# An adaLN linear-attention block with a token mixer: first modulation vectors and small inputs laid out in tiles of 128 partitions, half of their sum moved to TensorE

## The chip, the core and the metric

The kernel runs as one program on one core of a Trainium2 chip. The metric is the device time of one execution in microseconds (us); the median of three runs before the change is 452.39 us (452.24 to 452.70).

## The reference, cut to what matters

A block of 2048 tokens (S) by 448 channels (D). A condition vector c gives six modulation vectors; the first two, sa and ca, shape the input of the attention.

```python
mod = (silu(c) @ w_mod).reshape(1, 6, 1, 448)
sa, ca, ga, sb, cb, gb = (mod[:, i] for i in range(6))
h = layernorm(x) * (1 + ca) + sa
x = x + ga * linear_attention(h, wqkv, wo)        # 16 heads of 28, phi = elu + 1
h = layernorm(x) * (1 + cb) + sb
x = x + gb * mixer(h, w1, b1, w2, b2)             # W2 gelu(W1 h + b1) + b2 over the tokens
```

Inputs and output are float32. c has 448 numbers, w_mod is 448 x 2688, wqkv 448 x 1344.

## The kernel before, in words

The program is one long manual schedule: each engine runs its instructions in the order in which the Python code emits them, and waits only for data. Tokens are handled in 16 tiles of 128 (index t), channels in chunks of 128 (three full ones and one of 64, chunk index ch). Matrix products are done in float32 for the first tile (`project0`) and afterwards as sums of float32r products of a high and a low part (`split`, `project`, `a_outer`). Then come the token mixer's first product (w1, lines 740 to 742) and its second (w2, a Strassen-like scheme, lines 932 and 933).

What matters here is the head, everything before the first product of tile 0.

- **Loads.** SyncE (SP) issues them one after the other: c (line 99, four bytes apiece, to 112 partitions x 4), x tile 0 (`load_x`, line 104), four pieces of w_mod for vector 1, which is ca (`load_mod`, line 111, 112 partitions x 448 each), four pieces for vector 0, which is sa, x tile 1, then wqkv's k part (`load_qkv`, lines 119 and 122, the last 64 rows twice, each in a transfer of its own), x tile 2, wqkv's q part, x tiles 3 to 6. There are eight semaphores for these loads, used in turn, so that each load waits for the landing of the eighth load before it.
- **silu(c).** ScalarE (ACT) takes the exponential (`ec`, line 147), VectorE (DVE) does the rest (lines 149 to 151, result `sc`), and makes the broadcast columns `scb` of the last two pieces (line 425).
- **Modulation vectors.** For vector j, DVE multiplies the first three of the four pieces by their column of `sc` and adds them (`mod_acc`, lines 160 and 162, one pass of 112 x 448 for each). TensorE (PE) then sums over the partitions (`mod_sum`, line 177): one product of the fourth piece with its `scb`, and one of the accumulated tile with ones. Vector 1 is copied out of PSUM with 1 added (`mod_out`, line 156, tile `mods[1]`). Vector 0 stays in PSUM (`sap`) and is read from there by tile 0 and tile 1; it is copied out later, behind the work of tile 1.
- **Tile 0.** `a_stats` (lines 276 to 289; the power of -0.5 is on GpSimd, POOL), `a_norm_a` (line 294, needs `mods[1]`), `a_cols` (line 432, multiplies by the reciprocal deviation and adds sa, in two column pieces of 256 and 192), transposes on PE (`a_first`, line 437), copies by ACT (`a_copy`, line 442), and the first product kp (`project0`, line 448). Between its second and third chunk `project0` puts the transposes of tile 1 (`a_transpose`, line 312), which need `a_norm_a(1)`, `a_norm_b(1)` (line 300) and a small copy (`a_dup`, line 304).
- **Fillers.** `keep_warm` (line 141) issues 128 x 128 products of ones whose result nobody reads: 12 + 10 ahead of the first modulation sum, 5 ahead of the second, then twice 2. 

In code order, the head ends so (the names in the lines below recur in the steps):

```python
    a_stats(0)
    mod_acc(1, 3)
    keep_warm(WARM2)
    mod_out(1, mod_sum(1, 3))
    mod_acc(0, 3)
    keep_warm(WARM3)
    a_norm_a(0)
    moments1 = a_moments(1)
    a_stats(1, moments1)
    sap = mod_sum(0, 3)
```

From tile 0's first product on, the loop over tiles goes on with `project`, `a_outer`, `a_pk_parts` (POOL's accumulating DMAs at lines 376, 399 and 405) and, in iteration 4, the loads of wo, wqkv's v part, b1 and b2 (lines 582 and 584, four bytes apiece).

Of the kernel before, what the change touches and what calls it, by code (L numbers as in the profile page):

```python
# [32 lines left out]
QS = {0: 2, 4: 2}  # L33
WARM = 12
WARM2, WARM3 = 10, 5
ACT_STATS = ()
# [7 lines left out]
@with_exitstack  # L44
def block_kernel(ctx: ExitStack, tc: tile.TileContext, x, wqkv, wo, w1, b1, w2, b2, c, wmod, out):
    nc = tc.nc
# [25 lines left out]
    def bank(name):  # L72
        return psum.tile([P, 512], F32, name=name, tag="bank")
# [23 lines left out]

    c_sb = cst.tile([G, 4], F32, name="c_sb")
    nc.sync.dma_start(c_sb, c.rearrange("o (k p) -> p (o k)", p=G))
    X = [None] * NT  # L100

    def load_x(t):
        X[t] = slot(f"x{t}")
        nc.sync.dma_start(X[t], xf[t * P:(t + 1) * P, :])
# [10 lines left out]
    def load_qkv(j, new=None):  # L115
        new = new or slot
        for ch in range(3):
            raw_w[j, ch] = new(f"wr{j}_{ch}")
            nc.sync.dma_start(raw_w[j, ch], wqkv[ch * P:(ch + 1) * P, j * D:(j + 1) * D])
        raw_w[j, 3] = new(f"wr{j}_3")  # L120
        for h in range(2):
            nc.sync.dma_start(raw_w[j, 3][h * 64:(h + 1) * 64, :], wqkv[384:448, j * D:(j + 1) * D])

    load_x(0)
    load_mod(1)
    load_mod(0)
    load_x(1)
    load_qkv(1)
    load_x(2)
# [9 lines left out]
    def keep_warm(n):  # L139
        for i in range(n):  # L140
            nc.tensor.matmul(warm[:, :P], ones, ones, start=True, stop=True)
# [3 lines left out]

    ec = cst.tile([G, 4], F32, name="ec")
    nc.scalar.activation(ec, c_sb, AF.Exp, scale=-1.0)
    sc = cst.tile([G, 4], F32, name="sc")
    nc.vector.tensor_scalar_add(ec, ec, 1.0)
# [7 lines left out]

    def mod_acc(j, n=4):
        acc = (tslot if j == 5 else slot)(f"acc{j}", parts=G)
        nc.vector.tensor_scalar_mul(acc, wm[j, 0], sc[:, 0:1])  # L160
        for k in range(1, n):
            nc.vector.scalar_tensor_tensor(acc, wm[j, k], sc[:, k:k + 1], acc, op0=ALU.mult, op1=ALU.add)
        macc[j] = acc

    def mod_part(j, k):
        if k == 0:
            macc[j] = (tslot if j == 5 else slot)(f"acc{j}", parts=G)
            nc.vector.tensor_scalar_mul(macc[j], wm[j, 0], sc[:, 0:1])
        else:
            nc.vector.scalar_tensor_tensor(macc[j], wm[j, k], sc[:, k:k + 1], macc[j], op0=ALU.mult, op1=ALU.add)  # L170

    def mod_sum(j, n=4):
        ps = bank(f"modp{j}")
        todo = [(scb[:, (k - 2) * P:(k - 1) * P], wm[j, k]) for k in range(n, 4)]
        todo.insert(1, (ones[:G, :], macc.pop(j)))
        for k, (a, b) in enumerate(todo):
            nc.tensor.matmul(ps[:, :D], a, b, start=(k == 0), stop=(k == len(todo) - 1))
        return ps

# [242 lines left out]

    scb = cst.tile([G, 2 * P], F32, name="scb")
    for k in range(2):
        nc.vector.tensor_scalar_mul(scb[:, k * P:(k + 1) * P], ones[:G, :], sc[:, k + 2:k + 3])

# [3 lines left out]
    def a_cols(c0, c1, sa):  # L430
        h = hs[0]
        nc.vector.scalar_tensor_tensor(h[:, c0:c1], h[:, c0:c1], st[0][1], sa[:, c0:c1], op0=ALU.mult, op1=ALU.add)

# [30 lines left out]
    keep_warm(2)  # L464
    a_cols(0, 256, sap)
    a_cols(256, D, sap)
    tps[0] = bank("tp0")
# [10 lines left out]
    w_high(1, 1)  # L478
    a_norm_b(1, sap[:, :D])
    a_dup(1)  # L480
# [7 lines left out]
    w_low(1, 3)  # L488
    mod_out(0, sap)
    a_stats(2)  # L490
# [45 lines left out]
    for t in range(3, NT):  # L536
# [581 lines left out]

_INS = ['A_x', 'A_wqkv', 'A_wo', 'B_w1', 'B_b1', 'B_w2', 'B_b2', 'c', 'w_mod']
_OUTS = [((1, S, D), 'float32')]  # L1120


# [20 lines left out]
```

## Time and profile before

| | |
|---|---|
| median of 3 runs | 452.39 us (452.24 to 452.70) |
| profiled execution, first to last instruction (span) | 451.1 us |
| median of the runs over that span | 1.3 us |
| PE busy | 444.3 us, 98% of the span |
| DVE, ACT, POOL busy | 352.0, 255.7, 109.0 us |
| DMA, mean over the span | 137 GB/s |

The profile shows one execution on the hardware. A row names the line, the engine, the operation and its tiles; a chain of waits goes back from the last instruction to what released each step. PE rows overlap, since products are pipelined, and each float32 product appears as two rows. The profiled execution gives no whole time of its own besides its span; differences are formed on the span and carried over to the median.

### The profile page before, as it was taken

Reading aid. Unit: us, or ns where it says so; the run is one execution under the profiler, and the core shown is the slowest. Engines: PE = TensorE matmul, PEld = TensorE weight load, DVE = VectorE, ACT = ScalarE, POOL = GpSimd, SP = SyncE. Lnnn points to the kernel's source line nnn. Section 1 sums busy time; section 2 is a strip of 40 time slices with the busy share of each in tenths; the row PEclk is TensorE's granted clock in tenths of the full one; section 3 lists DMA queues with packets and bytes.
Section 4 is the critical chain, followed back from the end, with each engine's and each line's share of the span. In section 5 each row is a group of like instructions: output and inputs, shape, how many; then the busy total and the mean of one; then the engine's idle time right before and its main releaser. Section 6 shows DMA issues by size and latency. Waiting matters only on the chain.

```text
span 451.1 us, 7324 instructions
## 1 busy us (share of the span) xinstructions
PE 444.3 (98%) x2396; PEld 408.5 (91%) x2396; DVE 352.0 (78%) x767; ACT 255.7 (57%) x568; POOL 109.0 (24%) x186
## 2 busy tenths in 40 slices
PE   8999999999999999999999999999999999999996
PEld 7589999889899999999999999999999999999996
DVE  5797797789799899897559686639697888978873
ACT  2659877655666576767675454326554547356531
POOL 2124575520013345554300000000110211302101
PEclk9999999999999999999999999999999999999999
DMA  8959899995200002322317553317987569975334
GB/s 216 293 146 190 143 194 238 188 246 159 72 0 2 23 25 80 82 50 50 117 27 221 178 173 116 103 62 221 279 207 182 98 186 211 191 192 99 57 85 62
DMA packets 62246, 61.63 MB, mean 137 GB/s; under 512 B 9152, under 2 KB 54784, under 8 KB 62208
## 3 DMA queue, kind: packets, MB, share of 16 engines
q1 hardware_dynamic: 53136, 46.94, 35.8%
q0 software_dynamic: 9072, 14.23, 19.9%
q8 instruction: 19, 0.31, 0.3%
q14 instruction: 19, 0.16, 0.1%
HBM read 42.34 MB, written 7.34 MB: 110 GB/s over the span
## 4 chain that ended last, share of the span: by engine, by line
PE 86%; POOL 4%; issue 4%; DVE 2%; DMA 1%; SPq 1%; ACT 0%; POOLq 0%; DVEq 0%
PE y L932 14%; PE up L742 10%; PE up L741 10%; PE up L740 10%; PE op L689 9%; PE qp L333 7%; PE y L933 7%; PE cacc L420 3%; PE kp L333 3%; PE yp L740 2%; PE yp L742 2%; PE yp L741 2%; PE tq L673 2%; POOL xl L376 1%; DMA wm<-in_w_mod_dram 1%
## 5 line engine op out<-in xcount | busy, mean ns | idle before, releaser
L742 PE MATMUL up<-h2h,pl 128*128 128x448 f32 x224 | 81.3, 363 | 0.0
L741 PE MATMUL up<-h2l,ph 128*128 128x448 f32 x224 | 81.2, 362 | 0.0
L740 PE MATMUL up<-h2h,ph 128*128 128x448 f32 x224 | 80.8, 361 | 0.0
L741 PEld LDWEIGHTS up<-h2l,ph 128*128 128x128 f32 x224 | 42.1, 188 | 3.1
L740 PEld LDWEIGHTS up<-h2h,ph 128*128 128x128 f32 x224 | 41.9, 187 | 3.0
L742 PEld LDWEIGHTS up<-h2h,pl 128*128 128x128 f32 x224 | 42.1, 188 | 2.4
L77 DVE TENSOR_TENSOR pl<-pr,ph 128x512 fp32r<-128x512 f32 (+1 forms) x60 | 36.3, 616 | 8.6 <-ACT ph L76 6.1
L76 ACT ACTIVATE ph<-pr 128x512 fp32r<-128x512 f32 (+1 forms) x60 | 32.8, 569 | 13.2 <-PE up L741 6.8
L894 POOL DMA_DIRECT2D a<-a x12 | 11.2, 1070 | 110.3 <-PE yp L742 97.0
L952 POOL DMA_DIRECT2D out_dram<-yt x12 | 10.5, 873 | 85.7 <-DVE yt L943 57.3
L689 PE MATMUL op<-wph,pth 112*128 112x448 f32 x64 | 24.5, 382 | 0.0
L420 PE MATMUL cacc<-pkh,xh 128*128 128x448 f32 x64 | 24.3, 379 | 0.0
L689 PE MATMUL op<-wpl,pth 112*128 112x448 f32 x64 | 23.2, 363 | 0.0
L420 PE MATMUL cacc<-pkl,xh 128*128 128x448 f32 x64 | 23.2, 362 | 0.0
L689 PE MATMUL op<-wph,ptl 112*128 112x448 f32 x64 | 23.1, 362 | 0.0
L938 ACT ACTIVATE cc<-y 128x448 f32<-128x448 f32 x18 | 9.8, 544 | 23.3 <-PE y L933 23.3
L333 PE MATMUL kp<-wh,hl 128*128 128x448 f32 x60 | 21.7, 367 | 1.1 <-DVE hl L77 1.1
L333 PE MATMUL kp<-wh,hh 128*128 128x448 f32 x60 | 21.6, 366 | 0.0
L333 PE MATMUL qp<-wh,hh 128*128 128x448 f32 x60 | 21.6, 366 | 0.0
L333 PE MATMUL qp<-wh,hl 128*128 128x448 f32 x60 | 21.4, 363 | 0.0
L677 ACT ACTIVATE pth<-tq 112x512 fp32r<-112x512 f32 x16 | 9.6, 599 | 20.5 <-PE tq L673 17.7
L289 POOL TENSOR_TENSOR rs<-ve,mhalf 128x1 f32<-128x1 f32 x16 | 14.3, 896 | 24.5 <-DVE ve L287 23.9
(214 smaller groups left out, 1309.8 us busy)
## 6 DMA issues: line engine op xcount, KB each, us to landing
pr<-in_B_w_dram SPq DMA_DIRECT2D x48, 256.0 KB, 3.1
a<-in_B_w_dram SPq DMA_DIRECT2D x24, 256.0 KB, 5.0
wm<-in_w_mod_dram SPq DMA_DIRECT2D x24, 196.0 KB, 4.9
a<-in_B_w_dram SPq DMA_DIRECT2D x24, 192.0 KB, 5.0
x<-in_A_x_dram SPq DMA_DIRECT2D x16, 224.0 KB, 4.5
pk<-pk POOLq DMA_DIRECT2D x12, 224.0 KB, 5.0
out_dram<-x SPq DMA_DIRECT2D x12, 224.0 KB, 2.0
out_dram<-yt POOLq DMA_DIRECT2D x12, 224.0 KB, 4.2
```

Source lines behind the costliest of these rows:

```text
L76: nc.scalar.activation(hi, full, AF.Copy)
L77: nc.vector.tensor_sub(lo, full, hi.bitcast(F32))
L289: nc.gpsimd.tensor_tensor(rs, ve, mhalf[:, 0:1], op=ALU.pow)
L333: nc.tensor.matmul(o, a[:, ch * P:(ch + 1) * P], b, start=(n == 0), stop=(n == 10))
L420: nc.tensor.matmul(cacc[ch][:, :D], a[:, s], b, start=(t == 0 and i == 0), stop=(t == NT - 1 and i == len(todo) - 1))
L689: nc.tensor.matmul(opb[t][:, :D], a[:, s], b, start=(n == 0), stop=(n == 11))
L740: nc.tensor.matmul(ps[:, :D], hi[:, sl], mh, start=first, stop=False)
L741: nc.tensor.matmul(ps[:, :D], hi[:, sl], ml, start=False, stop=False)
L742: nc.tensor.matmul(ps[:, :D], lo[:, sl], mh, start=False, stop=last)
L894: nc.gpsimd.dma_start(w, a, accum_op=ALU.add)
L932: nc.tensor.matmul(ps[:, :D], h[:, s], w, start=opens and r == 0, stop=False, skip_group_check=True)
L933: nc.tensor.matmul(ps[:, :HD], l[:, s], wh, start=False, stop=closes and r == PAIRS - 1, skip_group_check=True)
```

## The change

The host lays out five inputs anew, and the kernel reads them in that form.

- c comes as 128 x 8: columns 0 to 2 are its chunks of 128, column 3 is the last 64 numbers twice, columns 4 to 7 are the four pieces of 112 (for the later vectors). Its load is issued by ACT, no longer by SP.
- The parts of w_mod for vectors 1 and 0 come as one array `first` of 2 x 128 x 1600: three chunks of 128 rows x 448, and a fourth in which the last 64 rows stand as 128 partitions x 256 (columns 0 to 255 on partitions 0 to 63, columns 256 to 447 on partitions 64 to 127, filled with zeros). SP loads vector 1 first, then x tile 0, vector 0, the first k chunk, x tile 1, the rest.
- wqkv comes as tiles of 128 x 448, its last 64 rows twice in one tile, hence one load in place of two; b1 and b2 come as 128 x 14 and 128 x 16.
- PE now sums chunks 0 and 1 of each vector directly (`spread`, `first_mm`); DVE handles chunk 2 and the folded chunk 3 alone (`first_acc`: one multiplication and two passes on 64 partitions). Vector 0 is summed in two PSUM banks (256 and 192 columns), each with its own piece of `first_acc`.
- Tile 1's moments stand behind `a_cols` instead of ahead of it, and `a_norm_b(1)` reads `mods[0]`, which ACT copies out of the two banks ahead of it; the later copy of vector 0 is gone.
- The fillers are 9, 3 and 2, in place of 12, 10 and 5.

```diff
-WARM = 12
-WARM2, WARM3 = 10, 5
+WARM = 9
+WARM2, WARM3 = 3, 2
...
-    c_sb = cst.tile([G, 4], F32, name="c_sb")
-    nc.sync.dma_start(c_sb, c.rearrange("o (k p) -> p (o k)", p=G))
+    c_sb = cst.tile([P, 8], F32, name="c_sb")
+    nc.scalar.dma_start(c_sb, c)
...
+    def load_first(j):
+        for k in range(4):
+            w = D if k < 3 else 256
+            wm[j, k] = slot(f"wm{j}_{k}", w)
+            nc.sync.dma_start(wm[j, k], wfirst[j, :, k * D:k * D + w])
+
+    load_first(1)
     load_x(0)
-    load_mod(1)
-    load_mod(0)
+    load_first(0)
+    load_qkv(1, chs=(0,))
     load_x(1)
-    load_qkv(1)
+    load_qkv(1, chs=(1, 2, 3))
...
+    def spread(k):
+        nc.vector.tensor_scalar_mul(scb[:, k * P:(k + 1) * P], ones, sc[:, k:k + 1])
+
+    def first_acc(j, c0, c1, rows):
+        if j not in macc:
+            macc[j] = slot(f"acc{j}")
+        acc = macc[j]
+        nc.vector.tensor_scalar_mul(acc[:, c0:c1], wm[j, 2][:, c0:c1], sc[:, 2:3])
+        for r in rows:
+            p, (d0, d1) = slice(r * 64, (r + 1) * 64), ((0, 256), (256, D))[r]
+            nc.vector.scalar_tensor_tensor(acc[p, d0:d1], wm[j, 3][p, :d1 - d0], sc[p, 3:4], acc[p, d0:d1],
+                                           op0=ALU.mult, op1=ALU.add)
+
+    def first_mm(j, k, ps, c0, c1):
+        a, b = (scb[:, k * P:(k + 1) * P], wm[j, k]) if k < 2 else (ones, macc[j])
+        nc.tensor.matmul(ps[:, :c1 - c0], a, b[:, c0:c1], start=k == 0, stop=k == 2)
...
+    ca = bank("modp1")
+    first_mm(1, 0, ca, 0, D)
+    first_mm(1, 1, ca, 0, D)
+    first_acc(1, 0, D, (0, 1))
+    keep_warm(WARM2)
+    first_mm(1, 2, ca, 0, D)
+    mod_out(1, ca)
+    del macc[1]
     a_stats(0)
-    mod_acc(1, 3)
-    keep_warm(WARM2)
-    mod_out(1, mod_sum(1, 3))
-    mod_acc(0, 3)
+    saps = [(bank("modp0"), 0, 256), (bank("modq0"), 256, D)]
+    for k in (0, 1):
+        for sap in saps:
+            first_mm(0, k, *sap)
+    a_norm_a(0)
+    for r, sap in enumerate(saps):
+        first_acc(0, *sap[1:], (r,))
     keep_warm(WARM3)
-    a_norm_a(0)
+    for sap in saps:
+        first_mm(0, 2, *sap)
+    del macc[0]
+    a_cols(0, 256, saps[0][0])
+    a_cols(256, D, saps[1][0])
     moments1 = a_moments(1)
     a_stats(1, moments1)
-    sap = mod_sum(0, 3)
-    keep_warm(2)
-    a_cols(0, 256, sap)
-    a_cols(256, D, sap)
...
     w_high(1, 1)
-    a_norm_b(1, sap[:, :D])
+    mods[0] = cst.tile([P, D], F32, name="mod0")
+    for ps, c0, c1 in saps:
+        nc.scalar.activation(mods[0][:, c0:c1], ps[:, :c1 - c0], AF.Copy)
+    a_norm_b(1)
...
-    mod_out(0, sap)
...
-            nc.sync.dma_start(b1c, b1.rearrange("(k p) -> p k", p=P))
+            nc.sync.dma_start(b1c, b1)
-            nc.sync.dma_start(b2c, b2.rearrange("(k p) -> p k", p=P))
+            nc.sync.dma_start(b2c, b2)
```

PE's head before, from its first filler to the first product of tile 0 (modp are the banks of the modulation sums, acc the tiles that DVE accumulates, wm_3 the fourth pieces, tp and kp tile 0's transposes and product):

```order
L141 MATMUL warm<-ones 128x128 x22
L177 MATMUL modp_185<-wm_3_100,scb 128x448
L177 MATMUL modp_185<-acc_171,ones 128x448
L141 MATMUL warm<-ones 128x128 x5
L177 MATMUL modp_209<-wm_3_108,scb 128x448
L177 MATMUL modp_209<-acc_190,ones 128x448
L141 MATMUL warm<-ones 128x128 x2
L437 MATMUL tp_216<-ident,h_199 128x128 x3
```

The same stretch of PE with the change (wm_0 and wm_1 are chunks 0 and 1; modp_179 and modq_180 the two banks of vector 0):

```order
L145 MATMUL warm<-ones 128x128 x9
L179 MATMUL modp_158<-wm_0_92,scb 128x448
L179 MATMUL modp_158<-wm_1_94,scb 128x448
L145 MATMUL warm<-ones 128x128 x3
L179 MATMUL modp_158<-acc_161,ones 128x448
L179 MATMUL modp_179<-wm_0_102,scb 128x256
L179 MATMUL modq_180<-wm_0_102,scb 128x192
L179 MATMUL modp_179<-wm_1_104,scb 128x256
L179 MATMUL modq_180<-wm_1_104,scb 128x192
L145 MATMUL warm<-ones 128x128 x2
L179 MATMUL modp_179<-acc_187,ones 128x256
L179 MATMUL modq_180<-acc_187,ones 128x192
```

Behind the last load of vector 0, PE now has two short products in place of two long ones, and the products with `scb` stand ahead of it.

DVE's rows from the last pieces of vector 0 to tile 1's normalisation, before (x_110 is tile 1's input, h_199 and h_228 are the normalised tiles 0 and 1):

```order
L162 SCALAR_TENSOR_TENSOR acc_190<-wm_2_106,sc,acc_190 112x448
L294 SCALAR_TENSOR_TENSOR h_199<-x_92,mv_165,mod_188 128x448
L276 BN_STATS st_201<-x_110 128x6
L285 BN_AGGR mv_203<-st_201 128x2
L287 TENSOR_SCALAR ve_205<-mv_203 128x1
L432 SCALAR_TENSOR_TENSOR h_199<-h_199,rs_169,modp_209 128x256
L432 SCALAR_TENSOR_TENSOR h_199<-h_199,rs_169,modp_209 128x192
L294 SCALAR_TENSOR_TENSOR h_228<-x_110,mv_203,mod_188 128x448
L300 SCALAR_TENSOR_TENSOR h_228<-h_228,rs_207,modp_209 128x448
```

The same place with the change (x_112 is tile 1's input, h_185 and h_218 the normalised tiles, mod_222 the copy of vector 0):

```order
L302 SCALAR_TENSOR_TENSOR h_185<-x_100,mv_173,mod_169 128x448
L171 TENSOR_SCALAR acc_187<-wm_2_106,sc 128x256
L174 SCALAR_TENSOR_TENSOR acc_187<-wm_3_108,sc,acc_187 64x256
L171 TENSOR_SCALAR acc_187<-wm_2_106,sc 128x192
L174 SCALAR_TENSOR_TENSOR acc_187<-wm_3_108,sc,acc_187 64x192
L439 SCALAR_TENSOR_TENSOR h_185<-h_185,rs_177,modp_179 128x256
L439 SCALAR_TENSOR_TENSOR h_185<-h_185,rs_177,modq_180 128x192
L284 BN_STATS st_198<-x_112 128x6
L293 BN_AGGR mv_200<-st_198 128x2
L295 TENSOR_SCALAR ve_202<-mv_200 128x1
L302 SCALAR_TENSOR_TENSOR h_218<-x_112,mv_200,mod_169 128x448
L308 SCALAR_TENSOR_TENSOR h_218<-h_218,rs_204,mod_222 128x448
```

Tile 0's h now needs nothing of tile 1, and tile 1's moments and both its passes stand behind tile 0's last one. The sum over chunk 2 and 3 of vector 0 waits behind tile 0's first normalisation pass.

ACT's rows at the start with the change (before, the third row was not there, and ec was the next row):

```order
L83 ACT_TABLE_LOAD
L83 ACTIVATE ones_r<-ones 128x128
L99 DMA c_sb<-in_c_dram 128x8
L151 ACTIVATE ec<-c_sb 128x8
L160 ACTIVATE mod_169<-modp_158 128x448
```

The load of c stands behind the table load and the copy of the ones on ACT.

More of the change, by code (lines that the diff above doesn't have):

```diff
@@ L44, in block_kernel @@
 @with_exitstack
-def block_kernel(ctx: ExitStack, tc: tile.TileContext, x, wqkv, wo, w1, b1, w2, b2, c, wmod, out):
+def block_kernel(ctx: ExitStack, tc: tile.TileContext, x, wqkv, wo, w1, b1, w2, b2, c, wmod, wfirst, out):
     nc = tc.nc
@@ L143, in block_kernel @@
     keep_warm(WARM)
-    ec = cst.tile([G, 4], F32, name="ec")
+    ec = cst.tile([P, 8], F32, name="ec")
     nc.scalar.activation(ec, c_sb, AF.Exp, scale=-1.0)
-    sc = cst.tile([G, 4], F32, name="sc")
+    sc = cst.tile([P, 8], F32, name="sc")
     nc.vector.tensor_scalar_add(ec, ec, 1.0)
@@ L156, in mod_out @@
         nc.scalar.activation(mods[j], ps[:, :D], AF.Copy, bias=1.0 if j in (1, 4) else 0.0)
[L158 to L163, printed above, removed]
+    scb = cst.tile([P, 2 * P], F32, name="scb")
+    def spread(k):
[12 more added lines that the diff above has]
+        nc.tensor.matmul(ps[:, :c1 - c0], a, b[:, c0:c1], start=k == 0, stop=k == 2)
     def mod_part(j, k):
@@ L167, in mod_part @@
             macc[j] = (tslot if j == 5 else slot)(f"acc{j}", parts=G)
-            nc.vector.tensor_scalar_mul(macc[j], wm[j, 0], sc[:, 0:1])
+            nc.vector.tensor_scalar_mul(macc[j], wm[j, 0], sc[:G, 4:5])
         else:
[L170 to L178, printed above, removed]
+            nc.vector.scalar_tensor_tensor(macc[j], wm[j, k], sc[:G, 4 + k:5 + k], macc[j], op0=ALU.mult, op1=ALU.add)
     def mod_split(j):
@@ L421, in a_outer @@
                                  stop=(t == NT - 1 and i == len(todo) - 1))
-    scb = cst.tile([G, 2 * P], F32, name="scb")
-    for k in range(2):
-        nc.vector.tensor_scalar_mul(scb[:, k * P:(k + 1) * P], ones[:G, :], sc[:, k + 2:k + 3])
+    spread(0)
+    spread(1)
     h0t = slot("h0t", 512)
```

42 lines of the change are left out of this document (33 added, 9 removed).

## Prediction

> **What bounds the kernel now.** I read the page first, then a table by stages, then PE's waits, then the chain of waits for the head.
>
> ```profile
> PE 444.3 (98%) x2396; PEld 408.5 (91%) x2396; DVE 352.0 (78%) x767; ACT 255.7 (57%) x568; POOL 109.0 (24%) x186
> ```
>
> PE is busy nearly everywhere, so only PE's waits and its head can be won. The table by stretches (busy time of each engine, then granted clock, DMA share, GB/s) shows where PE is not busy:
>
> ```profile
> 0.00:14.88 14.88, 13.13 (x74) 10.79 (x75) 8.73 (x24) 3.35 (x7) 3.73 (x11) 1.00 0.87 232
> 14.88:46.00 31.12, 31.12 (x146) 25.30 (x147) 25.77 (x57) 23.05 (x53) 9.50 (x12) 1.00 0.86 200
> 46.00:93.00 47.00, 45.50 (x241) 41.42 (x240) 37.16 (x84) 35.38 (x76) 28.37 (x37) 1.00 0.98 195
> ```
>
> From 14.88 to 46 us PE has no gap. From 46 to 93 it loses 1.50 us, and the view of PE's waits from 15 to 95 us names them:
>
> ```profile
> PE kp L333 <- DVE hl L77: 1.1, 2, 0.8
> PE tp L312 <- DVE h L300: 0.4, 1, 0.4
> ```
>
> Behind 95 us that view has no row. So PE's program from the first product of tile 0 on is rigid, and what the head gives is passed on to the end. In the head, PE's 13.13 busy us are mostly fillers; the chain of waits (start, length) shows what really ends it:
>
> ```profile
> 1.24 0.48 SPq L104
> ...
> 5.06 6.13 DMA wm<-in_w_mod_dram
> 11.19 0.04 issue
> 11.23 1.78 PE modp L177 x4
> ...
> 13.11 0.49 DVE h L432
> ...
> 14.88 1.77 PE kp L448 x4
> 16.65 0.44 PE tp L312 x4
> ```
>
> The last w_mod piece of vector 0 lands at 11.19. Then follow the two modulation products, `a_cols`, the transposes, and tile 0's product at 14.88. PE reaches tile 1's transposes at 16.65. I compare there, since there the change has its next wait.
>
> **The change part by part.** Three things decide: when the last piece of vector 0 lands (L), when c lands (C), and what lies behind them.
>
> *Behind L.* The DVE rows by form (busy, mean ns):
>
> ```profile
> L432 DVE SCALAR_TENSOR_TENSOR h<-h,rs,modp 128x256 f32<-128x256 f32 x1 | 0.5, 481 | 0.5 <-PE modp L177 0.5
> L432 DVE SCALAR_TENSOR_TENSOR h<-h,rs,modp 128x192 f32<-128x192 f32 x1 | 0.4, 408 | 0.0
> L160 DVE TENSOR_SCALAR acc<-wm,sc 112x448 f32<-112x448 f32 x2 | 0.9, 450 | 0.3 <-DMA wm<-in_w_mod_dram 0.3
> ```
>
> Before, `a_cols` ends at 13.11 + 0.81 (both pieces, which overlap by 0.08) = 13.92, 2.73 us behind L. With the change the folded chunk's pass on 64 x 256 has the width of the first row, 0.48; then the multiplication of 192 columns, some 0.2 by the third row's width; the pass on 64 x 192, 0.41: DVE is through at L + 1.1. PE's second-bank product follows: the rows of the products give 0.92 for 448 columns,
>
> ```profile
> 9.10 0.92 PE L177 MATMUL modp<-acc,ones 112*128 112x448 f32 x2
> 10.05 0.54 ACT L156 ACTIVATE mod<-modp 128x448 f32<-128x448 f32 x1 [6.90 <-PE modp L177]
> ```
>
> so about 0.6 for 256 and 0.5 for 192. The first bank's product runs beside DVE's second piece, the first `a_cols` beside the second bank's product, and the end of `a_cols` comes out at L + 1.1 + 0.1 + 0.5 + 0.4, that is L + 2.05. That is 0.68 less than before.
>
> *L itself.* The loads from issue to landing (size, us), each from the DMA view of its own issue, in the order x tile 0, the first, second and last piece of w_mod:
>
> ```profile
> x<-in_A_x_dram SPq DMA_DIRECT2D x1, 224.0 KB, 2.8
> wm<-in_w_mod_dram SPq DMA_DIRECT2D x1, 196.0 KB, 2.9
> wm<-in_w_mod_dram SPq DMA_DIRECT2D x1, 196.0 KB, 4.7
> wm<-in_w_mod_dram SPq DMA_DIRECT2D x1, 196.0 KB, 6.1
> ```
>
> Before, 224 + 8 x 196 = 1792 KB come from 1.24 to 11.19. With the change 2 x (3 x 224 + 128) + 224 = 1824 KB come from 0.80, the place of c's issue. At the same pace that is 9.95 x 1824 / 1792 = 10.13, L = 10.9. The other end: the stretch from 5 to 10 us moves 288 GB/s,
>
> ```profile
> 5.00:10.00 5.00, 4.69 (x33) 3.78 (x32) 2.65 (x7) 0.00 (x0) 0.71 (x1) 1.00 0.98 288
> ```
>
> and 0.80 + 2.8 for the first 224 KB and 1600 KB (1.64 MB) at 288 GB/s give L = 9.3. I take 10.5, nearer the first end, since queue and engines are the same.
>
> *C.* c moves from SP to ACT, behind two operations (single rows of the timeline, and of the DMA view the last):
>
> ```profile
> 0.79 1.28 ACT L83 ACT_TABLE_LOAD   x1 [0.79 <-PEq L1130]
> 2.08 0.31 ACT L83 ACTIVATE ones_r<-ones 128x128 fp32r<-128x128 f32 x1
> 2.94 0.20 ACT L147 ACTIVATE ec<-c_sb 112x4 f32<-112x4 f32 x1 [0.55 <-DMA c_sb<-in_c_dram]
> 3.60 0.16 DVE L151 TENSOR_TENSOR sc<-c_sb,ec 112x4 f32<-112x4 f32 x1
> 3.79 0.48 DVE L425 TENSOR_SCALAR scb<-ones,sc 112x128 f32<-112x128 f32 x2
> c_sb<-in_c_dram SPq DMA_DIRECT2D x1, 1.8 KB, 2.1
> ```
>
> The trace has no load issued by ACT. If ACT's queue sends it while the table loads, C stays at 2.9; if it waits for `ones_r` (2.39) and lands as late as the third of the four loads above, 2.39 + 4.7, C = 7.1. I take 2.39 + 2.1 = 4.5, rounded up to 4.7 for the loads beside it: its own row is the nearest. What hangs on c is longer than before, because PE now needs `scb` for its first product: `sc` at C + 0.9, first `scb` at C + 1.2, two products (0.75 apiece when issued back to back), three fillers (0.64), the third product (0.92), `mod_out` (0.54), tile 0's first pass (0.68) and the multiplication of chunk 2 (0.3): DVE is ready for the folded chunk of vector 0 at C + 5.8. With C = 4.7 that is 10.5, the same as L. So `a_cols` ends at 10.5 + 2.05 = 12.55, against 13.92: **1.37 us earlier**.
>
> The Trainium skill, "DMA: Bandwidth & Descriptors", section "Issuing engines are not separate DMA queues", says that transfers of all issuing engines share 16 DMA engines and interleave, so that ACT's queue gives c no free lane. By it C lies nearer 7.1 than 4.5 and the time nearer that of the late-c rival below; no run here shows it.
>
> *Behind `a_cols`, a new wait.* Tile 1's moments now follow it. The rows:
>
> ```profile
> 14.44 0.70 ACT L442 ACTIVATE h0t<-tp 128x256 f32<-128x256 f32 x3 [1.59 <-PE tp L437]
> 15.04 0.57 ACT L197 ACTIVATE wh<-wr 128x448 fp32r<-128x448 f32 x1
> 12.50 0.15 DVE L287 TENSOR_SCALAR ve<-mv 128x1 f32<-128x1 f32 x1
> 12.74 0.55 POOL L289 TENSOR_TENSOR rs<-ve,mhalf 128x1 f32<-128x1 f32 x1 [6.73 <-DVE ve L287]
> 14.61 0.68 DVE L300 SCALAR_TENSOR_TENSOR h<-h,rs,modp 128x448 f32<-128x448 f32 x1
> ```
>
> Call the end of `a_cols` T. DVE: moments from T to T + 0.95, first pass to T + 1.55. POOL's power: T + 1.6 (it took 0.55). ACT: the copies of tile 0 and `w_high(1, 1)` end at T + 1.6 (before, 15.61 against 13.92), then the two new copies of vector 0 (0.54 for 448 columns in one; some 0.6 in two): T + 2.15. So `a_norm_b(1)` starts at T + 2.2, takes 0.68, and tile 1 is ready at T + 2.9. PE is there at T + 2.73 (16.65 against 13.92). The new wait is 0.2. Queued behind it on PE are the rest of kp for tile 0 and all that follows; `a_dup` on ACT is hidden behind the first three transposes.
>
> *At nothing.* The later copy of vector 0 (0.54 on ACT at 18.1) is gone, but PE had no wait there. wqkv's loads lose two issues, but tile 0 does not wait for them: ahead of its copies ACT waits 1.59 for PE. b1 and b2 lose their four-byte pieces at 34 to 41 us: PE has no wait until 46 us, and the chain there goes back to PE itself. Without that cover (POOL's accumulating DMAs late) it would be worth at most the 1.5 us of waits above. PE's extra products lie ahead of L.
>
> **Sum.** 1.37 - 0.2 = 1.2 us. The profiled span would go from 451.1 to 449.9; the same off the median of 452.39, 1.3 above the span, gives **451.2**.
>
> **Rivals.**
>
> 1. *c is late.* With C = 6.1, C + 5.8 = 11.9, `a_cols` ends at 13.95 and the head gains nothing: 452.6 with the new wait. With C = 7.1 it is 453.6. Against it: c alone took 2.1. For it: several of SP's loads are under way by then.
>
> 2. *The loads get faster* (128 rows of 1792 B in one block, no four-byte pieces ahead of them). With L = 9.3 and C below 3.5, `a_cols` ends at 11.35, 2.57 earlier: 450.0. For it: x tile 0, such a load, landed in 2.8 beside 4.7 for the second piece of w_mod. Against it: the DMA share is already 0.98 from 5 to 10 us.
>
> 3. *Slower: PE's clock rises late.* The fillers' rows at 1 to 4 us and at 5 to 8 us (min/median/max, first and last start):
>
> ```profile
> L141 PE MATMUL warm<-ones x13: 421/421/583, 1.1 to 3.8; 128*128 128x128 f32 x13
> L141 PE MATMUL warm<-ones x27: 275/275/275, 4.8 to 7.7; 128*128 128x128 f32 x27
> ```
>
> Twelve steps in 2.7 us are 0.225 each, then 26 in 2.9 us, 0.11: PE doubles its pace some 3 us after it starts. Nine fillers are 18 rows, 4.0 us, and end at 5.1 if nothing rises, only a little beyond the change of pace; then PE waits for c. If the pace rises only later, the two products and three fillers behind c cost 2.3 us more, and the third product another 0.8. Then vector 1 comes at C + 5.8 + 2.3 to 3.1 = 12.8 to 13.6, `a_cols` at 14.85 to 15.65: 453.5 to 454.3, say 453.9. It decides from the point where PE's nine fillers end before the pace changes. The Trainium skill, "TensorE: Matmul & The Clock Gate", part 1, puts the rise at about 3.4 us of sustained work, in windows that run free of the kernel's start. The rows agree with the length; by the free phase an execution may miss its window, which would make this case one of some runs.
>
> 4. *The gain is eaten on the way.* POOL and ACT carry the chain from 46 to 92 us; were they tied to transfers and not to PE, the end would stay: 452.4. Against it: both waits of PE there are on DVE's results, and DMA comes to rest between (200 GB/s from 14.88 to 46, with a share of 0.86).
>
> **How the numbers follow.** Forecast (450.7 to 451.7) 0.50; faster loads 0.15; late c 0.20; late clock 0.10; eaten 0.05. A difference of 0.2%, 0.9 us, is about what a measurement of this kernel tells from none: faster means below 451.5, slower above 453.3. Of the forecast 0.40 lies below 451.5; with rival 2 faster is 0.55. Slower is the late clock and 0.03 of the late c, 0.13. The rest, 0.32, is the same. The range from 450.2 to 452.9 holds the forecast, most of rivals 1 and 2, and rival 4; it leaves out the late clock and the ends of the two bounds.
>
> **What would show it.** In the changed profile: the last `first` load lands at 9.3 to 10.9; ACT's `ec` starts below 5; `a_cols` ends near 12.5 and tile 1's transposes start near 15.5, with a wait of some 0.2 on DVE's h; the fillers' rows are at 275 ns from 4.8 on. The forecast is wrong if `ec` starts beyond 6, if rows of 421 ns stand behind 5.5, or if PE's waits behind 46 us grow by what the head gains.

## The result and the profile after

The changed kernel takes **451.57 us** (median of 19 executions, 450.09 to 452.78) against 452.39 (19 executions, 451.10 to 453.94): ratio **0.9981, 95% interval 0.9971 to 0.9991**, that is 0.4 to 1.3 us faster, forecast 1.2. Run again beside other executions of the kernel before it gave 451.83 and 0.9990 (0.9973 to 1.0006). The two intervals overlap; a gain of some 0.6 us fits both.

The profiled spans are 451.1 before and 449.1 after, 2.0 apart, which is more than the times. The profile of the kernel before is a long one: of its 105 later executions with a span on record only 5 reach 451.1, and their medians are 450.0 to 450.4. The same table by stretches, cut at tile 0's first product (now at 13.89 us, before 14.88):

```profile
0.00:13.89 13.89, 12.51 (x55) 9.55 (x55) 7.38 (x24) 3.36 (x8) 3.04 (x10) 1.00 0.86 276
13.89:46.00 32.11, 31.84 (x149) 25.64 (x150) 27.07 (x58) 23.40 (x55) 10.96 (x13) 1.00 0.73 185
46.00:93.00 47.00, 46.52 (x247) 42.69 (x246) 38.21 (x85) 35.91 (x78) 28.62 (x36) 1.00 1.01 205
```

The 1.00 of the first row counts time without a clock record as full; the first record, of the full clock, stands at 6.84 us. PE's waits from 13.8 to 100 us name what is left:

```profile
PE tp L320 <- DVE h L308: 0.3, 1, 0.3
PE kp L341 <- DVE hl L77: 0.3, 1, 0.3
PE cacc L428 <- DMA pkl<-pk: 0.2, 1, 0.2
```

The first row is the new wait at tile 1's transposes. From 46 to 93 us PE now loses 0.48 us where it lost 1.50. The same products in both profiles, before and after, at 80 us and at the end:

```profile
80.44 0.36 PE L333 MATMUL kp<-wh,hh 128*128 128x448 f32 x1
79.98 0.36 PE L341 MATMUL kp<-wh,hh 128*128 128x448 f32 x1
446.18 1.49 PE L1007 MATMUL yl<-uw,qw 128*128 128x224 f32 x12
444.49 1.49 PE L1027 MATMUL yl<-uw,qw 128*128 128x224 f32 x12
```

So of the 2.0 us, the head gave 0.46 (the first outer product starts at 34.04 instead of 34.50, and the distance is the same at 80 us), the stretch from 81 to 95 us, where PE's other waits stand, 1.24, and what follows PE's last product 0.3. The experiments show which of these belong to the change.

The chain of waits for the head (in part, as marked):

```profile
1.11 4.21 PE warm L145 x18
5.32 2.32 PE modp L179 x4
7.64 0.67 PE warm L145 x6
8.31 0.77 PE modp L179 x2
...
9.10 0.55 ACT mod L160
...
10.28 0.36 DVE acc L171
...
10.66 0.49 DVE acc L174
...
11.20 0.71 PE modp L179 x2
...
12.00 0.49 DVE h L439
...
14.15 0.46 ACT wh L205
14.62 0.49 ACT mod L499 x2
...
15.19 0.70 DVE h L308
...
15.93 0.66 PE tp L320 x4
```

Before, this chain went through the landing of vector 0's last piece. In this profile no load stands in it now. It is PE working on vector 1 from its fillers on, then the copy on ACT (9.10), tile 0's first pass, vector 0's two pieces and `a_cols`, which ends at 12.92. A second profile of the same kernel (after_again) has another chain, which begins with the landing of vector 1's third piece at 6.64 us:

```profile
1.71 4.93 DMA wm<-in_first_dram
...
6.66 0.47 DVE acc L171
```

The loads themselves, vector 1's third piece (issued at 1.71) and vector 0's last (issued at 4.55), in the first profile, from the DMA view (size, us to landing):

```profile
wm<-in_first_dram SPq DMA_DIRECT2D x1, 224.0 KB, 4.3
```

```profile
wm<-in_first_dram SPq DMA_DIRECT2D x1, 128.0 KB, 4.5
```

They land at 6.0 and 9.1 us. Before, vector 0's last piece landed at 11.19. And c's load, with the first operation that uses it:

```profile
1.09 0.41 ACTq L99 DMA_DIRECT2D c_sb<-in_c_dram  x1
...
3.63 0.21 ACT L151 ACTIVATE ec<-c_sb 128x8 f32<-128x8 f32 x1 [1.24 <-DMA c_sb<-in_c_dram]
```

### The profile page after: what moved, and what is told of

The parts are those of the page before. It is cut to its first block, busy times and chain, and to the rows that moved or that the text cites. A ratio compares the mean times of both kernels' runs of the same rounds, so it can differ in the third digit from the quotient of the medians.

```text
span 449.1 us, 7278 instructions
## 1 busy us (share of the span) xinstructions
PE 443.8 (99%) x2376; PEld 407.4 (91%) x2376; DVE 351.5 (78%) x768; ACT 256.0 (57%) x569; POOL 108.8 (24%) x186
## 4 chain that ended last, share of the span: by engine, by line
PE 96%; DVE 1%; issue 1%; ACT 1%; POOL 0%; DVEq 0%; POOLq 0%
PE y L952 14%; PE up L762 10%; PE up L761 10%; PE up L760 10%; PE op L709 9%; PE qp L341 7%; PE kp L341 7%; PE cacc L428 7%; PE y L953 7%; PE yp L760 2%; PE yp L762 2%; PE yp L761 2%; PE tq L693 2%; PE tp L320 1%; PE warm L145 1%; PE modp L179 1%
## 5 line engine op out<-in xcount | busy, mean ns | idle before, releaser
L972 POOL DMA_DIRECT2D out_dram<-yt x12 | 10.5, 873 | 84.6 <-DVE yt L963 56.2
```

## The experiments

Twelve kernels ran. Three sets of four shared their executions of the kernel before: after_again, b_old, b_only and no_fill2 one set (median of the kernel before 451.74), mod0_first, c_on_sp, dve_sum and k23_first the next (452.07), dve_sum_warm, old_pieces, k23_mod0 and fill_moved the last (451.87). Each ratio is to those executions and not the quotient of the two medians, from which it differs by up to 0.0012 (after_again); medians of different sets can't be compared. The readings from each kernel's one profile (us):

| kernel | vector 1's sum on DVE starts | vector 1's copy | end of `a_cols` | first outer product | median time | ratio (95%) |
|---|---|---|---|---|---|---|
| before | 5.13 | 10.05 | 13.91 | 34.50 | 452.39 | 1 |
| after | 6.06 | 9.10 | 12.92 | 34.04 | 451.57 | 0.9981 (0.9971 to 0.9991) |
| after_again | 6.66 | 9.17 | 12.99 | 34.11 | 451.83 | 0.9990 (0.9973 to 1.0006) |
| b_old | 6.51 | 9.02 | 12.84 | 33.96 | 451.51 | 0.9985 (0.9973 to 0.9998) |
| b_only | 5.11 | 9.81 | 13.64 | 34.23 | 451.68 | 0.9993 (0.9980 to 1.0005) |
| no_fill2 | 6.50 | 9.01 | 12.84 | 33.97 | 450.85 | 0.9974 (0.9961 to 0.9987) |
| mod0_first | 6.12 | 9.38 | 13.20 | 34.04 | 450.85 | 0.9976 (0.9967 to 0.9984) |
| c_on_sp | 6.65 | 9.16 | 12.98 | 34.10 | 451.09 | 0.9984 (0.9974 to 0.9993) |
| dve_sum | 4.56 | 8.67 | 13.77 | 35.63 | 452.22 | 1.0005 (0.9996 to 1.0014) |
| dve_sum_warm | 4.53 | 8.94 | 13.35 | 34.47 | 451.06 | 0.9982 (0.9973 to 0.9991) |
| old_pieces | 6.37 | 8.70 | 13.27 | 34.39 | 451.10 | 0.9990 (0.9978 to 1.0003) |
| k23_first | 4.95 | 8.46 | 12.29 | 33.41 | 450.40 | 0.9974 (0.9960 to 0.9987) |
| k23_mod0 | 4.95 | 9.17 | 13.00 | 33.83 | 450.87 | 0.9983 (0.9970 to 0.9995) |
| fill_moved | 6.41 | 8.91 | 12.85 | 33.97 | 451.00 | 0.9985 (0.9971 to 1.0000) |

### Once more, and b1 and b2 apart

after_again is the changed kernel; b_old has the old loads of b1 and b2 in it; b_only has the new loads of b1 and b2 in the kernel before. The edit of b_old, which b_only makes the other way round:

```diff
-            nc.sync.dma_start(b1c, b1)
+            nc.sync.dma_start(b1c, b1.rearrange("(k p) -> p k", p=P))
-            nc.sync.dma_start(b2c, b2)
+            nc.sync.dma_start(b2c, b2.rearrange("(k p) -> p k", p=P))
```

> The changed kernel once more, for a second profile. Theory A (PE's own chain from c ends the head: nine fillers, two products at whatever pace the clock has, three fillers, the third product): the pace rises at another moment than the 6.84 us of the first profile; if it rises near 4.6, a_cols ends about 0.8 us sooner than the 12.92 there (near 12.1), tile 1's transposes start near 15.2, if it rises near 6.8 they start near 15.9 again. Rival L (the loads end the head): the end of a_cols follows the landing of vector 0's last piece and not the clock. For the stretch behind 46 us: theory B (the four-byte loads of b1 and b2 held POOL's transfers back before) says PE's waits there stay near the 0.5 us of the first profile of the change; the rival, chance from one execution to the next, says anything from 0.4 to 1.5.

> The changed kernel with b1 and b2 loaded four bytes apiece again, nothing else undone. Theory B: PE's waits behind 46 us are back at about 1.5, against 0.5 with the change, and the time is about 1 us above the changed kernel's 451.6, near 452.5. Rival (chance, or another part of the change): the waits are within what the changed kernel itself shows and the time stays at 451.6. In both, SP's issue of x tile 9 comes some 3 us later again and the head is as in the changed kernel.

> The kernel before, with b1 and b2 alone laid out by the host. Theory B: tile 1's transposes at 16.65 as before, PE's waits behind 46 us fall from 1.5 to about 0.5, time near 451.4. Rival: the waits vary as they do in the kernel before, time 452.4.

PE's waits on `hl` from 14 to 100 us, in after_again, b_old and b_only, one row each:

```profile
PE kp L341 <- DVE hl L77: 0.8, 1, 0.8
```

```profile
PE kp L341 <- DVE hl L77: 0.7, 1, 0.7
```

```profile
PE kp L333 <- DVE hl L77: 0.4, 1, 0.4
```

The theory that the four-byte loads hold back this stretch falls. With the new loads the wait is 0.3, 0.8 or 0.4, with the old ones 0.7 or (before) 1.1, and b_old's time cannot be told from after_again's, nor b_only's from that of before. The wait varies between executions. b_only, whose head is that of before, gains 1.56 us on the first profile from 81 to 95 us, more than the changed kernel's 1.24, so nothing shows that the 1.24 is the change's.

after_again bears on the head too. Its full clock is first recorded at 5.98 us, 0.86 sooner than in the first profile, yet `a_cols` ends at 12.99, no sooner; in b_old, whose head is the same, it is recorded at 4.13, and `a_cols` ends at 12.84. In both, vector 1's third piece landed later than in the first profile (6.6 and 6.5 for 6.0), and the chain of waits begins there. That speaks against theory A.

### The three fillers

```diff
-WARM2, WARM3 = 3, 2
+WARM2, WARM3 = 0, 2
```

> The changed kernel without the three fillers ahead of vector 1's third product. Theory A: these fillers stand on the path (0.64 us at the fast pace, 1.35 at the slow one, less what DVE's second folded pass needs), so vector 1, tile 0's first pass and the end of a_cols come 0.5 to 0.7 us sooner at the same clock, time near 451.0; the pace still rises, since the products take the fillers' place. Rival L: the end of a_cols stays, time 451.6. A third possibility: PE idles enough that the pace rises one window later, then the time is 452 or more.

PE's rows by form up to 9 us, in after and in no_fill2 (busy, mean ns, idle ahead of them):

```profile
L145 PE MATMUL warm<-ones 128*128 128x128 f32 x24 | 5.0, 391 | 1.1 <-DVE mhalf L95 1.1
L179 PE MATMUL modp<-wm,scb 128*128 128x448 f32 x4 | 2.5, 778 | 0.0
L179 PE MATMUL modp<-acc,ones 128*128 128x448 f32 x2 | 0.9, 540 | 0.0
```

```profile
L179 PE MATMUL modp<-wm,scb 128*128 128x448 f32 x4 | 1.8, 565 | 0.1
L179 PE MATMUL modp<-acc,ones 128*128 128x448 f32 x2 | 1.0, 591 | 1.3 <-DVE acc L174 1.3
```

and DVE's row in no_fill2 that the sum starts with:

```profile
6.50 0.45 DVE L171 TENSOR_SCALAR acc<-wm,sc 128x448 f32<-128x448 f32 x1 [1.46 <-DMA wm<-in_first_dram]
```

In after, PE's pace rose late (the first record of the full clock is at 6.84 us), its first two products took 778 ns a row for 565, and PE with the fillers was last, some 0.7 us behind DVE's sum. In no_fill2 the pace rose at 4.09, PE stood idle 1.3 us for DVE, and DVE 1.46 for vector 1's third piece, which landed at 6.5 instead of 6.0. `a_cols` ends at 12.92 and 12.84. So my theory for this set, that PE's own chain from c alone ends the head, falls, and so does the rival that vector 0's last piece does. **Two chains end close to each other: PE's, when its pace rises late, and the one from the landing of vector 1's third piece.** Which is last changes from one execution to the next (in after_again PE, with its fillers, waited 0.2 us for DVE), and taking away one shows the other. The median of 450.85 is where theory A had put it, but most of the distance to after_again's 451.83 lies outside the profiled span (see the last experiment).

### The wait at tile 1's transposes

```diff
     a_norm_a(1)
-    w_high(1, 1)
     mods[0] = cst.tile([P, D], F32, name="mod0")
     for ps, c0, c1 in saps:
         nc.scalar.activation(mods[0][:, c0:c1], ps[:, :c1 - c0], AF.Copy)
+    w_high(1, 1)
     a_norm_b(1)
```

> The changed kernel with ACT's two copies of vector 0 put ahead of the high half of wqkv's second chunk, instead of behind it. Theory (the new wait at tile 1's transposes is made by ACT's order): in the changed kernel DVE's last pass on tile 1 stands 0.73 us for these copies and PE 0.27 us for it, then 0.22 us for the duplicated columns; the copies come 0.57 us earlier, so both waits of PE go and everything behind comes 0.3 to 0.5 us sooner: about 451.2 if the changed kernel is at 451.6. Rival: the high half of the second chunk, 0.7 us later now, becomes the next thing PE waits for ahead of tile 1's first product, and the time stays (451.6).

DVE's last pass on tile 1, in after and in mod0_first:

```profile
15.19 0.69 DVE L308 SCALAR_TENSOR_TENSOR h<-h,rs,mod 128x448 f32<-128x448 f32 x1 [0.73 <-ACT mod L499]
```

```profile
15.18 0.69 DVE L308 SCALAR_TENSOR_TENSOR h<-h,rs,mod 128x448 f32<-128x448 f32 x1 [0.45 <-POOL rs L297]
```

The copies no longer stand ahead of it; POOL's power for tile 1 does now. Tile 1's transposes start 2.72 us behind `a_cols` (13.20 to 15.92) instead of 3.01, and PE has no wait there. That is 0.3 us, the low end of what was expected, and the rival (the second chunk's high half becomes late) is out; k23_mod0, with the same move, has 2.72 too. The transposes start no sooner than in after (15.93), since here `a_cols` ends 0.28 later, for another reason: vector 1's fourth piece landed late, at 7.3 us.

```profile
7.36 0.91 DVE L174 SCALAR_TENSOR_TENSOR acc<-wm,sc,acc 64x256 f32<-64x256 f32 x2 [0.79 <-DMA wm<-in_first_dram]
```

The 0.22 us that the expectation gave to the duplicated columns is no wait: in after the four transposes start at 15.93, 16.09, 16.20 and 16.31 us, one right behind the other. The interval of the ratio overlaps that of after, so the gain stands in the profile and not in the times.

### c on SP again

```diff
-    nc.scalar.dma_start(c_sb, c)
+    nc.sync.dma_start(c_sb, c)
```

> The changed kernel with c issued by SP again, ahead of its loads, as in the kernel before. Theory D (what sets the head is, by turns, the landing of vector 1's third piece, PE's fillers where its pace rises late, and only behind them the last piece): each of SP's loads goes out 0.44 us later, vector 1's third piece lands at 6.5 to 6.9, a_cols ends 0.2 to 0.4 us later, at 13.1 to 13.3, and the time is 0.2 to 0.4 above the changed kernel's. Rival (the loads are held by their sum of bytes, not by the issue): a_cols stays at 12.9 and the time too. Beside it: if c on ACT's queue is what puts 2.4 to 3.1 us instead of 1.7 between span and time in about half of the changed kernel's executions, this kernel shows 1.7 in all and a median 0.4 lower for that.

```profile
2.53 0.21 ACT L151 ACTIVATE ec<-c_sb 128x8 f32<-128x8 f32 x1
```

c is in use at 2.53 us instead of 3.63, with no wait on its load. Vector 1's third piece lands at 6.65, as theory D said; `a_cols` ends at 12.98, a little below the 13.1 to 13.3 that it gave, and the time is that of after within the intervals. A c that comes 1.1 us sooner is worth nothing, since DVE's sum waits for the third piece all the same; the 0.44 us by which SP's loads go out later cost less than executions differ.

### DVE sums all, without and with fillers

The layout, the two banks and the order of the loads stay; DVE sums all four pieces, and PE does one product for each bank. dve_sum_warm has 12, 3 and 10 fillers besides.

```diff
+        nc.vector.tensor_scalar_mul(macc[j], wm[j, 0], sc[:, 0:1])
+        for k in (1, 2):
+            nc.vector.scalar_tensor_tensor(macc[j], wm[j, k], sc[:, k:k + 1], macc[j], op0=ALU.mult, op1=ALU.add)
...
-        a, b = (scb[:, k * P:(k + 1) * P], wm[j, k]) if k < 2 else (ones, macc[j])
-        nc.tensor.matmul(ps[:, :c1 - c0], a, b[:, c0:c1], start=k == 0, stop=k == 2)
+        nc.tensor.matmul(ps[:, :c1 - c0], ones, macc[j][:, c0:c1], start=True, stop=True)
...
-WARM = 9
-WARM2, WARM3 = 3, 2
+WARM = 12
+WARM2, WARM3 = 3, 10
```

> The changed kernel's layout, loads, two banks and later copy are kept, but DVE sums all chunks of the first two vectors and PE does one product for each bank. Theory (what the head wins is DVE's passes given to PE): vector 1 is through on DVE at about 8.1 us and its copy starts at 9.1 as now, but vector 0's three passes then lie between tile 0's statistics and its last pass, so the end of a_cols goes from 12.9 to about 13.6 and the gain is given back: 452.2 to 452.4. Rival (the laid-out loads make the gain, since the last piece lands 2.1 us earlier, at 9.1 for 11.2): a_cols ends at 12.9 to 13.0 and the time stays at 451.6.

> DVE sums all chunks as before in this study, but PE's gaps are filled: 12 fillers at the start, and 10 instead of 2 ahead of vector 0's products. In the run without them PE stood 1.0 and 2.4 us, and its granted clock fell to half from 10.2 to 17.0 us. Theory (that dip is a good part of what DVE's sum cost): the two products take 0.7 and 0.6 us for 1.2 and 0.85, a_cols ends at 13.2 to 13.4 instead of 13.8, tile 0's product starts 1.0 us behind it instead of 1.4, and the time is 0.4 to 1.0 below that run's ratio of 1.0005: 0.998 to 0.9995. Rival (the dip belongs to that one profile, and DVE's passes cost it all): the ratio stays at 1.0005.

The stretches of dve_sum, then of dve_sum_warm (the granted clock is the third number from the end):

```profile
6.73:10.15 3.42, 1.46 (x6) 0.90 (x6) 3.23 (x8) 0.95 (x2) 0.71 (x1) 1.00 1.08 355
10.15:16.97 6.82, 5.50 (x15) 3.75 (x16) 4.72 (x12) 1.81 (x7) 0.93 (x1) 0.50 1.02 372
```

```profile
6.73:10.15 3.42, 2.26 (x15) 1.89 (x16) 3.20 (x9) 0.75 (x2) 0.71 (x1) 1.00 1.01 354
10.15:16.97 6.82, 5.62 (x30) 3.58 (x30) 5.58 (x13) 2.65 (x9) 0.92 (x1) 1.00 1.04 383
```

and tile 0's products from 9 to 16 us in the same order:

```profile
L452 PE MATMUL kp<-wr,h0t 128*128 128x448 f32 x2 | 1.7, 954 | 0.0
```

```profile
L452 PE MATMUL kp<-wr,h0t 128*128 128x448 f32 x4 | 1.8, 565 | 0.0
```

By its time dve_sum had said that PE's half of the sum makes the whole gain. The profile says otherwise: PE was busy 1.46 of 3.42 us from 6.73 to 10.15, and the clock was then granted at 0.50 for 6.82 us, in which a product of tile 0 took 954 ns instead of 565. With fillers in these gaps the clock stays, and the ratio is 0.9982: DVE alone sums as well, as far as the times can tell. In the profile `a_cols` ends at 13.35 for 12.84 to 12.99, 0.4 us later, and its chain of waits runs over DVE from the third piece's landing (6.11) to 11.7; a difference of that size the times do not resolve. **So PE's half is worth some 0.4 us in the profile; the fillers that keep the clock are worth more** (1.0005 against 0.9982, intervals apart). The dip is not that one profile's alone. 6.82 us at half clock in a span of 450 make a mean of 0.992, and the profiled execution has it:

```profile
core 0: 450.0 us, clock 0.992
```

The mean granted clock is 0.988 to 0.992 in ten of dve_sum's eleven executions and 0.996 in the other, which is the shortest; no execution of another variant or of the kernel before is below 0.996.

### The old cut of the pieces

Pieces of 112 rows, four to a vector, not folded; all else as in the change.

```diff
-            wm[j, k] = slot(f"wm{j}_{k}", w)
-            nc.sync.dma_start(wm[j, k], wfirst[j, :, k * D:k * D + w])
+            wm[j, k] = slot(f"wm{j}_{k}", parts=G)
+            nc.sync.dma_start(wm[j, k], wmod[k * G:(k + 1) * G, j * D:(j + 1) * D])
```

> The changed kernel with the pieces of the first two vectors cut as before: 112 rows of w_mod at a time, four to a vector, not folded; PE still sums two of the four, vector 0 still has two banks, and the order of loads and work is that of the change. Theory (the pieces of 128 rows land sooner: before, 1792 KB took until 11.2 us, now 1824 KB until 9.1): vector 1's third piece lands at 6.9 to 7.5 us instead of 6.0 to 6.5, DVE's unfolded pass gives back 0.25, a_cols ends at 13.3 to 13.7, and most of the gain is gone: 0.9995 to 1.001 of the kernel before. Rival (the cut does not matter, the order of the loads and PE's share do): the third piece lands at 6.0 to 6.5, a_cols ends at 12.6, and the time is that of the changed kernel or 0.2 below: 0.9975 to 0.998.

DVE's rows for both vectors:

```profile
6.37 0.45 DVE L170 TENSOR_SCALAR acc<-wm,sc 112x448 f32<-112x448 f32 x1 [1.26 <-DMA wm<-in_B_wmod_dram]
6.90 0.68 DVE L171 SCALAR_TENSOR_TENSOR acc<-wm,sc,acc 112x448 f32<-112x448 f32 x1
...
11.00 0.48 DVE L171 SCALAR_TENSOR_TENSOR acc<-wm,sc,acc 112x256 f32<-112x256 f32 x1 [0.43 <-DMA wm<-in_B_wmod_dram]
```

Vector 1's third piece lands as early as in the change, at 6.3, and its unfolded pass is shorter (0.68 for 0.91), so that its copy starts at 8.70. So far the rival is right. But vector 0's last piece lands at 10.9, nearly as before the change, and now it is what DVE waits for: `a_cols` ends at 13.27. The theory had the wrong piece and the right end. The time lies between before and after and is told from neither. What the layout does is shown in the landings: the last piece comes at 9.1 to 10.0 in all eleven profiles with the new pieces, at 10.9 to 11.2 in the three with the old ones. This kernel also reads its pieces from w_mod itself, so it does not tell the 128 rows and the fold from the place in memory.

### Vector 1's pieces in another order

No fillers, the pieces of vector 1 loaded third, fourth, first, second; k23_mod0 has ACT's copies moved as well.

```diff
-    load_first(1)
+    load_first(1, (2, 3, 0, 1))
```

> The changed kernel without the three fillers behind vector 1's first two products, and with vector 1's pieces loaded in the order third, fourth, first, second, so that DVE's part comes ahead of PE's. Theory D: DVE sums its half at 5.1 to 6.5 us while the first two pieces still come; they land at 6.0 to 6.5, PE's three products end near 7.9 to 8.3, vector 1's copy starts near 8.2 instead of 9.0, and a_cols ends at 12.1 to 12.3 instead of 12.85: 0.5 to 0.7 us below the kernel without the fillers, some 450.3. Rival (the last piece of vector 0, landed at 9.1, or tile 0's statistics set the head): a_cols stays at 12.8 and the time at 450.9.

> The two edits that helped, together: no fillers behind vector 1's first two products, vector 1's pieces loaded third, fourth, first, second, and ACT's two copies of vector 0 ahead of the high half of wqkv's second chunk. Theory: a_cols ends at 12.3 as without the move of the copies, and tile 1's transposes follow 2.7 us behind it instead of 3.0, as the move alone showed; PE's first outer product comes at 33.1 for 33.4, and the time is 0.2 to 0.3 below that of the reordered loads alone: 0.9970 of the kernel before or less. Rival: with a_cols earlier, POOL's power for tile 1 (0.93 us, and already what DVE stood 0.45 us for) sets tile 1's last pass, and nothing is added: 0.9974.

PE's wait ahead of its first two products, first in k23_first and then in k23_mod0:

```profile
PE modp L179 <- DMA wm<-in_first_dram: 0.7, 1, 0.7
```

```profile
PE modp L179 <- DMA wm<-in_first_dram: 1.3, 1, 1.3
```

DVE's part is out of the way by 6.4 us in both, and then PE waits for the piece that is now loaded third. It landed at 5.7 in one profile and at 6.5 in the other: `a_cols` ends at 12.29, as expected, and at 13.00, which is no gain. The order changes who waits for vector 1's third load, not when it lands, and that moves by 0.8 us between executions. k23_first has the lowest median, 450.40, but its interval, 0.9960 to 0.9987, takes in that of after, and k23_mod0's 0.9983 does not confirm it. No version here is shown to beat the changed kernel.

### Time outside the span

fill_moved has the three fillers ahead of vector 0's last products.

```diff
-WARM2, WARM3 = 3, 2
+WARM2, WARM3 = 0, 5
```

> The changed kernel with its three fillers moved from behind vector 1's first two products to ahead of vector 0's last ones, so that PE has exactly as many instructions as in the changed kernel. Asked here is what puts 2.4 to 3.1 us instead of 1.7 between span and time in about half of the executions of the changed kernel, of the one with the old b1 and b2 loads, of the one with moved copies and of the one with c on SP. If it is the length of PE's program, this kernel shows both values; if it is the fillers at that place, it shows 1.7 alone, as the kernel without them. The head as without the fillers: a_cols ends at 12.85.

The difference of time and span was 1.65 to 1.85 us in all 105 executions of the kernel before in the three sets. In after it is above 1.9 in 9 of 19 and reaches 3.1; in after_again in 8 of 12. It goes with PE's program, whose matmuls the page counts (first row after, second no_fill2):

```profile
PE 443.8 (99%) x2376; PEld 407.4 (91%) x2376; DVE 351.5 (78%) x768; ACT 256.0 (57%) x569; POOL 108.8 (24%) x186
```

```profile
PE 442.5 (98%) x2370; PEld 405.7 (90%) x2370; DVE 351.5 (78%) x768; ACT 255.9 (57%) x569; POOL 108.8 (24%) x186
```

The changed kernel in both its sets and the five variants with 2376 show it (after, after_again, b_old, mod0_first, c_on_sp, fill_moved, old_pieces: 44 of 88 executions above 1.9). The six variants with 2364, 2370, 2386 or 2396 never do (71 executions, none above 1.85). Neither c's queue nor the fillers' place makes it, since c_on_sp and fill_moved show it too. By the medians it takes 0.7 us from after_again: its span is 449.35 (2.5 under its time), that of before in the same set 450.0 (1.7 under). It also makes no_fill2 look better than it is: its median time is 1.0 us below after_again's, its median span (449.15) only 0.2. By the spans the changed kernel gains 0.65 us in this set. Why that length of program costs time outside the span stays open.

## Why the prediction was right, step by step

- **The sum (1.2 us, 451.2).** Measured 0.8 by the medians, 0.4 to 1.3 by the interval; that is just under the 0.9 us (0.2%) from which the prediction calls a kernel faster. The direction and the place were right: `a_cols` ends 0.9 to 1.0 us earlier in the profiles, 0.43 of it is lost at tile 1's transposes and 0.1 up to the first outer product, and what is left is passed along unchanged up to 81 us. But that is 0.46 us (0.39 in after_again, 0.54 in b_old), well under half of the 1.2. The interval holds both, and what the head gave is not resolved by the times: that the median came out as near as 0.8 is in part luck, and the parts were less good than the sum.
- **L, vector 0's last piece, taken at 10.5.** It landed at 9.09, 0.2 below the lower end that I gave it; in the other ten profiles with these pieces it came at 9.1 to 10.0. 1824 KB in 8.3 us are 220 KB a us, against 180 before; old_pieces, with the old cut, gives 10.9 again. I leaned to the pace of before "since queue and engines are the same"; the layout of the pieces was what differed. So the loads got faster as the second rival had it, but its price of 2.57 us did not come, because DVE was not ready for the piece.
- **DVE ready for it at C + 5.8.** This step failed. C was 3.6 (forecast 4.7), so DVE would have been ready at 9.4; it was at 10.6. In the first profile the 1.2 us are PE's: its nine fillers ended at 5.11, 0.3 behind the first `scb`, and the two products took 2.4 until the next fillers, at the late pace, where I had put 1.5. But the chain from c also left out that vector 1's own third piece has to land (6.0 to 6.6) and that DVE's three operations on it (1.4 us) lie between. With PE's pace sooner that alone leads to nearly the same end: in after_again, b_old, no_fill2, c_on_sp and fill_moved the chain of waits begins with this landing. c_on_sp shows that c does not matter. That DVE's pass on the folded piece started at 10.66, so near the 10.5, is luck: c came 1.1 sooner than forecast and the chain behind it was 1.2 longer. The error in L, 1.4, does not count in the end, since DVE came later.
- **L + 2.05 for the end of `a_cols`.** The four terms as printed add to 2.1. From DVE's pass on the folded piece at 10.66 to 12.92 are 2.26, so they were right to 0.2. With the 0.16 by which that pass started behind 10.5, `a_cols` gained 0.99 in the profiles, not 1.37.
- **The new wait of 0.2.** Tile 1 was ready 2.96 us behind `a_cols` (15.88), forecast 2.9 (ACT's copies, 15.61 against 13.92, are 1.7 and not the 1.6 of the sum, so its own rows give 3.0). But PE was there earlier than I had it: before, the first transpose starts at 16.49, 2.58 behind `a_cols`, and I had taken the 16.65 of the chain of waits, which is the modelled end of the products ahead. The transposes now start 3.01 behind `a_cols`, so the wait costs 0.43, not 0.2, though the view of waits prints 0.27. `a_dup` was rightly called hidden.
- **Edits at nothing.** b1 and b2 (b_only 0.9993, b_old 0.9985) and the later copy of vector 0 were rightly left out.
- **The slow rival, a late clock.** Its condition came true in after (778 ns a row, full clock first recorded at 6.84 us, the last fillers at 4.9 us still at 421 ns where the prediction looked for 275), its price did not: `a_cols` ends 0.08 us later than in b_old, which has the same head and whose clock rose at 4.13 and whose third piece landed 0.4 later. The pace rose while the two products ran, so they and the fillers took 0.9 us more and not 2.3, and DVE, with vector 1's third piece, was ready only 0.7 before PE. The Trainium skill, "TensorE: Matmul & The Clock Gate", part 1, says that windows of some 3.4 us run free of the kernel's start, and the first records of the full clock, anywhere from 4.1 to 6.8 us with PE's first row always at 1.11, agree with it: they spread over 2.8 us, less than one such window.
- **c on ACT's queue.** c went out at 1.09 us, while the table load ran from 0.79, and was in use 2.5 us later; ahead of SP's loads (c_on_sp) it took 1.7 at most. So it was delayed by at least 0.8 beside the other loads, and did not take the 4.7 of the upper bound. The Trainium skill, "DMA: Bandwidth & Descriptors", section "Issuing engines are not separate DMA queues", says that loads of all engines interleave; the trace agrees in kind, and the use that I made of it, C nearer 7.1, was wrong.

## What to carry to other kernels

Follow back each operand of a chain's first product, not the one that the change speaks of: here c was moved, and in most profiles a weight piece loaded beside it set the start. When an edit takes matmuls away from a start-up, look at the granted clock of the next 10 us before its time is read as the cost of the edit. Where two chains end less than 1 us apart, taking time off one shows the other, and the times of single variants can then no longer rank them.

## What the runs showed of the hardware that was not expected

- With PE busy 1.46 of 3.42 us, the granted clock fell to 0.50 for the next 6.82 us, in the middle of a head that had already reached full clock (dve_sum). The mean clock shows a dip of this size or more in ten of that kernel's eleven executions.
- Pieces of 128 rows by 448 columns, and a last one folded to 128 by 256, landed at 199 to 220 KB a us from the first issue on (eleven profiles), the 112-row pieces at 177 to 185 (three), with the same queue.
- Half of the executions of kernels with 2376 matmul rows carry up to 1.2 us more outside the span than any other kernel of this study shows.
